# Small additions and scale products moved to GpSimd, and a new hand-planned order, in a fused attention and mixing kernel

## The chip, the cores and the metric

The kernel runs on one core of one Trainium2 chip. A core has TensorE (PE in the profile, matrix products and transposes into PSUM; PEld is its loading of weights), VectorE (DVE), ScalarE (ACT), GpSimd (POOL) and SyncE (SP), which mainly issues transfers. Each engine works through its own queue in the order in which the program issued its instructions; semaphores make one engine wait for another. The metric is the device time of one execution in microseconds. Before the change it is 216.95 us, the median of three runs (216.09 to 218.91).

## What is computed

The reference in numpy, cut to what matters; B = 4 batches, H = 4 heads, S = 1088 positions, D = 32, r = 8:

```python
def phi(x):                                   # 8 x 8 products of two sketches
    a = einsum('rd,bhsd->bhsr', S1, x)
    b = einsum('rd,bhsd->bhsr', S2, x)
    return einsum('bhsi,bhsj->bhsij', a, b).reshape(..., 64)
q_p, k_p = phi(q), phi(k)
kv  = einsum('bhsf,bhsd->bhfd', k_p, v)
z   = sum(k_p, axis=2)
num = einsum('bhsf,bhfd->bhsd', q_p, kv)
den = einsum('bhsf,bhf->bhs', q_p, z) + 1e-06
x   = (num / den) as (B, S, 128)
theta = x @ w_theta
y = w_tok_r @ (x * cos(theta)) + w_tok_i @ (x * sin(theta))   # mixes the 1088 positions
u = x + y
out = u + maximum(u @ w_ch, 0)
```

The denominator comes near zero for some positions, so the kernel keeps it in several exact pieces of the number ("levels"); w_tok arrives as 64-bit floats and is unpacked on the chip.

## The kernel before

Positions are cut into nine chunks of 128 (NC = 9, the last one padded), and three chunks make a group. Per batch the kernel goes through these stages, named here as the plan names them:

- **loads** of K, Q and V (576 KB each) on SP's queue, the first two K on ACT's; for batches 1 to 3 K is loaded a second time (loadh), and a rounded copy is added to it by a GpSimd transfer (`join`, L326).
- **grid / keys / sums / rest**: `key_sums` (L610) squares K on ACT, sums the squares over the partitions on PE, and takes from the sum a grid of powers (`key_grid`, L632: two products on ACT, then their negatives on GpSimd). K is rounded and split on DVE, and PE forms K'K per head in many small products.
- **kT / kf / kv**: `kfeatures` (L700): K transposed, sketched, its 64 features formed on DVE (one outer product per group), and kv summed on PE.
- **chain / kvb**: `chain` (L768) turns K'K into the vector z of the denominators in exact pieces; it reads the grid `kg`. `chain_out` (L866) makes the small factors `mk` and the epsilons `ep` on GpSimd.
- **qscale / qT / q0**: `query_scale` (L918) finds a power of two for Q: square on ACT, sum on PE, bits on DVE, and a product by 2^-49 on ACT (L938), which gives `qs`. `query_slices` transposes Q and multiplies it by `qs` on ACT, and DVE splits it in two.
- **levels / den**: `levels` (L966) multiplies Q with the sketches and with z on PE, then forms the denominators on DVE. `finish_den` (L1011) adds the epsilon, adds the two halves of the denominator (both 128x36) and takes the reciprocal, which then divides the first sketch.
- **num / theta / mix / out**: `outputs_x` (L1023) forms the features of Q (DVE), transposes them (PE), multiplies them with kv, and makes the angles, cosines and sines. `mix_row` (L1193) mixes the positions of batches 0 and 1 with 17 rows of w_tok (`row0` to `row16`, each 1088 KB, unpacked by two instructions of ACT and two of DVE); batches 2 and 3 share seven products instead of eight (`winograd`, L1287: m1 to m7, sums of weights ac1 to ac4). At the end of each comes u @ w_ch, the relu, a transpose and the store.

The work of all these stages is first recorded as 1003 steps ("op": an engine, a planned time, a function, and the buffers that it writes and reads). No scheduler runs: `ORDER` (L34) is the order of all steps, written out by hand or found beforehand, and `Layout.issue` walks through it. So the position of a step in `ORDER` sets its place in its engine's queue. `SLOTS` (L80) gives each buffer its place in eight classes of memory (22 "big" of 128x1152 floats, 5 "zs", 5 "hf", 8 PSUM banks "ps" and so on); a step that opens a buffer waits for the last users of that place. [...]

```python
GAPS = {11: 3, 57: 3, 79: 3, 110: 1, 203: 8, 153: 1, 77: 5, 86: 2, 163: 1}
...
for o in self.order:
    for _ in range(GAPS.get(o.i, 0)):
        fill()
    ...
    o.fn()
```

Most operations are issued through helpers, so that their lines in the profile are those of the helpers: L312 for two-input operations, L316 for tensor with scalars, L319 for both, L332 for matmuls.

Of the kernel before, what the change touches and what calls it, by code (L numbers as in the profile page):

```python
# [245 lines left out]
def kernel(  # L246
# [64 lines left out]
    def tt(eng, o, a, b, f):  # L311
        eng.tensor_tensor(out=o, in0=a, in1=b, op=f)  # L312
# [21 lines left out]
    def bc(x, axis, shape):  # L334
        return x.unsqueeze(axis).to_broadcast(shape)
# [274 lines left out]
    def key_sums(b):  # L610
# [20 lines left out]

        def key_grid():  # L632
            A.mul(kg[b]()[:, 0:1], pg()[:, 0:1], 2.0**5)
            A.mul(kg[b]()[:, 1:2], pg()[:, 0:1], 2.0**14)

        op("A", 0.28, key_grid, [(kg[b], 0)], [pg])
        op("G", 0.2, lambda: ts(kg[b]()[:, 2:4], kg[b]()[:, 0:2], -1.0, ALU.mult, eng=G), [(kg[b], 1)], [(kg[b], 0)], lk=1)

        def key_step():
            x = km()[:, 0:1]  # L640
            ts(x.bitcast(I32), km()[:, 1:2].bitcast(I32), 1, ALU.logical_shift_right)
            ts(x, x, 2.0**76, ALU.mult)

# [274 lines left out]
    def query_scale(b):  # L918
# [13 lines left out]
        def scale():  # L932
            ai = m()[:, 1:2].bitcast(I32)
            ts(ai, ai, 1, ALU.logical_shift_right, EXPO, ALU.bitwise_and)
            ts(ai, ai, EXPO, ALU.bitwise_xor)

        op("V", 0.36, scale, [m], [], lk=2)
        op("A", 0.2, lambda: A.mul(s()[:, 0:1], m()[:, 1:2], 2.0**-49), [(s, 0)], [m])  # L938

    def query_slices(b):  # L940
        at("qT", b)
# [537 lines left out]
```

## Time and profile before

| | |
|---|---|
| median of three runs | 216.95 us |
| the profiled execution | 215.9 us |
| its span, first to last instruction | 214.1 us |
| granted TensorE clock, mean | 0.999 |
| moved by transfers | 37.06 MB, 173 GB/s in the mean |

The profile is of one execution. Its page gives the busy time of each engine, then the span in 40 slices with the busy tenths of each, then the chain of work that ended last. Groups of instructions read: line, engine, operation, output tile <- input tiles, shapes, count | busy microseconds, mean nanoseconds of one | idle time before them and what ended it. Timeline rows read: start, duration, engine, line, operation, tiles, shapes, count, and in brackets the engine's idle time before and what ended it. A matmul of 32-bit floats stands in two records, so the 2140 records of PE are fewer instructions. As matmuls are pipelined and their ends modelled, a busy PE may hide short stalls.

### The profile page before, as it was taken

What the parts mean: (1) busy time and instruction counts of PE and PEld (TensorE: products, weight loads), DVE (VectorE), ACT (ScalarE), POOL (GpSimd) and SP (SyncE); (2) the same over time, 40 slices, a digit from 0 to 9 for tenths busy, and PEclk for the clock granted to TensorE, in tenths of its full rate; (3) what the DMA queues carried; (4) which work ended last, traced back from release to release, by engine and by line L of the source; (5) the groups of instructions that cost most, each with busy time, mean ns of one, the idle gap of its engine ahead of it and who ended that gap; (6) DMA issues with size and microseconds to landing.
All of it is one profiled execution on the core that took longest, in us unless ns stands there. A gap on an engine that the chain in (4) does not pass through costs nothing.

```text
span 214.1 us, 5301 instructions
## 1 busy us (share of the span) xinstructions
PE 207.0 (97%) x2140; PEld 149.7 (70%) x2140; DVE 180.7 (84%) x359; ACT 113.4 (53%) x240; POOL 37.2 (17%) x87
## 2 busy tenths in 40 slices
PE   7899999999999999999999999999999999999992
PEld 7677798968867676775665776666676776676682
DVE  1799999999999998997999999988579599995232
ACT  4899999999998986697531333149700000000000
POOL 1272740306400000840003010000040020020002
PEclk9999999999999999999999999999999999999999
DMA  6999999996996994093000443120590011213503
GB/s 222 393 417 418 384 368 418 420 341 120 357 281 214 431 423 201 29 330 72 0 0 7 69 117 106 32 39 22 174 161 0 0 40 27 40 37 52 92 0 67
DMA packets 28780, 37.06 MB, mean 173 GB/s; under 512 B 21332, under 2 KB 23812, under 8 KB 26580
## 3 DMA queue, kind: packets, MB, share of 16 engines
q1 hardware_dynamic: 23268, 31.91, 42.7%
q0 software_dynamic: 1488, 3.15, 7.0%
q10 hardware_dynamic: 4000, 1.67, 3.0%
q8 instruction: 17, 0.28, 0.5%
q14 instruction: 7, 0.06, 0.1%
HBM read 29.84 MB, written 4.00 MB: 158 GB/s over the span
## 4 chain that ended last, share of the span: by engine, by line
PE 55%; DVE 18%; issue 11%; ACT 6%; DMA 6%; POOL 1%; SPq 1%; POOLq 0%; DVEq 0%; ACTq 0%
PE ps L332 49%; DVE big L312 7%; DMA zs<-far 3%; DMA st<-s 2%; PE ps L1053 2%; PE ps L951 2%; ACT big L626 2%; DVE big L319 1%; DMA far<-zs 1%; DVE g L312 1%; DVE zs L312 1%; DVE big L316 1%; ACT g L726 1%; PE ps L361 1%; POOL out L1236 1%
## 5 line engine op out<-in xcount | busy, mean ns | idle before, releaser
L332 PE MATMUL ps<-big,zs 128*128 128x384 f32 (+2 forms) x380 | 108.9, 435 | 0.3 <-DVE zs L312 0.3
L332 PEld LDWEIGHTS ps<-big,zs 128*128 128x128 f32 x380 | 67.1, 190 | 34.8 <-issue 0.9
L1277 ACT COPY g<-ps 80x256 f32<-80x256 f32 x1 | 0.4, 368 | 55.4 <-PE ps L1270 55.4
L332 PE MATMUL ps<-big,big 128*32 128x32 f32 (+2 forms) x352 | 21.8, 234 | 0.0
L312 DVE CUSTOM_DVE_ANT_0 big<-big,big 128x2176 uint16<-128x2176 uint16 x17 | 21.6, 1282 | 0.1
L578 ACT ACTIVATE big<-zs 128x1088 int32<-128x1088 uint32 (+1 forms) x18 | 21.4, 1193 | 0.4 <-DVE g L312 0.4
L576 ACT ACTIVATE big<-zs 128x1088 f32<-128x1088 f32 x17 | 20.8, 1225 | 0.7 <-DVE lv L312 0.5
L332 PEld LDWEIGHTS ps<-big,big 128*32 128x32 f32 (+1 forms) x352 | 14.9, 124 | 5.6 <-issue 1.0
L312 DVE TENSOR_TENSOR big<-big,big 128x544 f32<-128x544 f32 x24 | 16.7, 714 | 0.1
L326 POOL DMA_DIRECT2D g<-big x6 | 5.3, 1071 | 56.2 <-ACT g L1213 56.2
L312 DVE TENSOR_TENSOR zs<-zs,g 128x384 f32<-128x384 f32 (+2 forms) x24 | 9.9, 450 | 4.7 <-DMA zs<-far 4.7
L1236 POOL DMA_DIRECT2D out<-g x6 | 3.8, 633 | 49.7 <-DVE g L1240 31.8
L316 DVE TENSOR_SCALAR big<-big 128x1088 int32<-128x1088 int32 x17 | 12.3, 721 | 0.0
L361 PE MATMUL ps<-idle 128*128 128x112 bf16 (+1 forms) x67 | 10.0, 312 | 1.3 <-POOL idle L363 1.3
L312 DVE TENSOR_TENSOR g<-lv 128x768 f32<-128x768 f32 x12 | 11.2, 950 | 0.1
L312 DVE TENSOR_TENSOR big<-big,hf 128x1152 f32<-128x1152 f32 x8 | 10.7, 1351 | 0.0
L332 PE MATMUL ps<-mf,big 128*128 128x96 f32 (+1 forms) x72 | 10.0, 277 | 0.4 <-DVE big L312 0.4
L332 PE MATMUL ps<-sbk,g 128*128 128x64 f32 x72 | 10.0, 276 | 0.3 <-ACT g L726 0.3
L332 PE MATMUL ps<-w,big 128*128 128x128 f32 (+1 forms) x76 | 10.2, 278 | 0.0
L1139 ACT ACTIVATE g<-g 128x384 f32<-128x384 f32 x12 | 6.3, 531 | 6.9 <-DVE g L319 6.9
L332 PEld LDWEIGHTS ps<-w,big 128*128 128x128 f32 (+1 forms) x76 | 9.4, 189 | 0.5
L332 PEld LDWEIGHTS ps<-sbk,g 128*128 128x128 f32 x72 | 9.0, 191 | 0.8 <-ACT g L726 0.6
(198 smaller groups left out, 352.9 us busy)
## 6 DMA issues: line engine op xcount, KB each, us to landing
zs<-w_tok SPq DMA_DIRECT2D x17, 1088.0 KB, 10.6
big<-k_l SPq DMA_DIRECT2D x5, 576.0 KB, 12.5
big<-v_l SPq DMA_DIRECT2D x4, 576.0 KB, 15.5
big<-q_l SPq DMA_DIRECT2D x3, 576.0 KB, 10.4
big<-hf POOLq DMA_DIRECT2D x3, 576.0 KB, 10.1
far<-zs SPq DMA_DIRECT2D x3, 576.0 KB, 4.4
zs<-far SPq DMA_DIRECT2D x12, 144.0 KB, 4.2
big<-k_l ACTq DMA_DIRECT2D x2, 576.0 KB, 4.4
```

The source lines that it names most:

```text
L312: eng.tensor_tensor(out=o, in0=a, in1=b, op=f)
L316: (eng or V).tensor_scalar(out=o, in0=a, scalar1=s1, scalar2=s2, op0=op0, **kw)
L326: op("G", 0.9, lambda: G.dma_start(dst(), src(), accum_op=ALU.add), w, r, fly=fly)
L332: T.matmul(o, lhs, rhs, start=start, stop=stop, skip_group_check=True)
L361: T.matmul(nowhere()[:, :n], idle()[:, 0:P], idle()[:, :n], start=True, stop=True, skip_group_check=True)
L576: op("A", 0.22 + n * 0.0009, lambda: A.activation(dfn(), words_of(raw(), n)[1].bitcast(F32), AF.Prelu, scale=2.0**-112, alpha=-(2.0**32)), ...
L578: op("A", 0.22 + n * 0.0009, lambda: A.activation(stp(), words_of(raw(), n)[0].bitcast(U32), AF.Copy, scale=2.0**-29), [stp], [raw])
L626: op("A", act(n) + 0.1, lambda: A.activation(flat(r()), kc(), AF.Square, accum_out=km()[:, 1:2]), [r, (km, 1)], [kx])
L951: T.transpose(tr()[:, i * P:(i + 1) * P], x()[:, g * GC + i].rearrange("p h d -> p (h d)"), ident())
L1053: T.transpose(tr()[:, i * P:(i + 1) * P], qp()[:, i * H + 2 * n:i * H + 2 * n + 2].rearrange("p h i j -> p (h i j)"), ident())
L1139: op("A", act(GW), lambda cs=cs: A.activation(cs()[:, 0], cs()[:, 1], AF.Abs), [(cs, 0)], [(cs, 1)])
L1236: E.dma_start(out[b, s0:s0 + n, f * SQ:(f + 1) * SQ].rearrange("(c j) i -> j c i", j=SQ), ot()[f * SQ:(f + 1) * SQ, :n].rearrange("j (c i) ...
```

## The change

Four things are edited.

1. `key_grid` keeps one product on ACT; the second grid value is made from the first by a GpSimd product (by 2^9), in front of the negatives, which were there already.
2. The product by 2^-49 in `query_scale` goes from ACT to GpSimd.
3. The two additions of `finish_den` go from DVE to GpSimd; the reciprocal becomes a step of its own on DVE. This adds one step per batch, 1007 in all, so that later steps have higher numbers in the new `ORDER`.
4. `ORDER` and `SLOTS` are replaced. The first 58 entries of `ORDER` are the same. `GAPS` is untouched; its keys are all below the first new step.

```diff
         pg = buf("ps", (512,), F32, "pg")
         op("P", 0.25, lambda: mm(pg()[:, 0:1], ones(), km()[:, 1:2], True, True), [pg], [(km, 1)])

-        def key_grid():
-            A.mul(kg[b]()[:, 0:1], pg()[:, 0:1], 2.0**5)
-            A.mul(kg[b]()[:, 1:2], pg()[:, 0:1], 2.0**14)
-
-        op("A", 0.28, key_grid, [(kg[b], 0)], [pg])
-        op("G", 0.2, lambda: ts(kg[b]()[:, 2:4], kg[b]()[:, 0:2], -1.0, ALU.mult, eng=G), [(kg[b], 1)], [(kg[b], 0)], lk=1)
+        def more_grid():
+            ts(kg[b]()[:, 1:2], kg[b]()[:, 0:1], 2.0**9, ALU.mult, eng=G)
+            ts(kg[b]()[:, 2:4], kg[b]()[:, 0:2], -1.0, ALU.mult, eng=G)
+
+        op("A", 0.2, lambda: A.mul(kg[b]()[:, 0:1], pg()[:, 0:1], 2.0**5), [(kg[b], 0)], [pg])
+        op("G", 0.7, more_grid, [(kg[b], 1)], [(kg[b], 0)], lk=2)
...
-        op("A", 0.2, lambda: A.mul(s()[:, 0:1], m()[:, 1:2], 2.0**-49), [(s, 0)], [m])
+        op("G", 0.5, lambda: ts(s()[:, 0:1], m()[:, 1:2], 2.0**-49, ALU.mult, eng=G), [(s, 0)], [m], lk=1)
...
         def finish_den():
             d1 = dn()[:, 1].rearrange("p (c h) -> p c h", h=H)
-            tt(V, d1, d1, bc(ep[b]()[:, 1], 1, [P, NC, H]), ALU.add)
-            tt(V, dn()[:, 0], dn()[:, 0], dn()[:, 1], ALU.add)
-            V.reciprocal(dn()[:, 1], dn()[:, 0])
-
-        op("V", 0.8, finish_den, [dn], [(ep[b], 1)], lk=2)
+            tt(G, d1, d1, bc(ep[b]()[:, 1], 1, [P, NC, H]), ALU.add)
+            tt(G, dn()[:, 0], dn()[:, 0], dn()[:, 1], ALU.add)
+
+        op("G", 0.55, finish_den, [dn], [(ep[b], 1)], lk=2)
+        op("V", 0.4, lambda: V.reciprocal(dn()[:, 1], dn()[:, 0]), [dn], [])
...
 ORDER = (
     0, 1, 29, 32, 4, 2, 5, 3, 34, 30, 356, 50, 33, 102, 44, 96, 6, 108, 103, 36, 7, 51, 366, 54, 144, 8, 97, 10, 9,
     11, 55, 109, 20, 52, 12, 57, 139, 58, 59, 60, 61, 62, 63, 126, 13, 31, 132, 56, 98, 127, 264, 14, 391, 128, 143,
-    245, 15, 145, 64, 65, 67, 68, 78, 35, 69, 16, 70, 19, 148, 149, 150, 151, 152, 268, 99, 66, 79, 246, 53, 80, 100,
...
+    245, 15, 145, 129, 99, 16, 104, 268, 130, 120, 100, 133, 246, 257, 78, 64, 65, 66, 105, 110, 111, 258, 19, 67, 53,
...
```

In the new order, behind the shared opening, the key features of batches 0, 1 and 3 (kT, kf, kv) come ahead of the small products of batch 0 (sums, rest), those of batch 1 (sums) come after them, and the squares of Q2 and K2 on ACT come ahead of the first unpacked row. On SP's queue the second copies of K2 and K3 and part of Q3 come earlier, and rows 11, 13, 15 and 16 of w_tok come last. Later, 41 instead of 36 mixing steps of batches 0 and 1 stand ahead of the levels of batch 3 on PE. At the very end the last output pieces of batches 2 and 3 change places: m4 instead of m3 is the last product.

103 rows, old and new, of tables (ORDER, SLOTS) are left out of this document.

## The prediction

> **What bounds the kernel now.** I read the page first, then the busy time in ten-microsecond windows, then what TensorE waited for, then the timeline of the places that the edits touch. From the page:
>
> ```profile
> span 214.1 us, 5301 instructions
> PE 207.0 (97%) x2140; PEld 149.7 (70%) x2140; DVE 180.7 (84%) x359; ACT 113.4 (53%) x240; POOL 37.2 (17%) x87
> PE   7899999999999999999999999999999999999992
> DVE  1799999999999998997999999988579599995232
> ACT  4899999999998986697531333149700000000000
> PE 55%; DVE 18%; issue 11%; ACT 6%; DMA 6%; POOL 1%; SPq 1%; POOLq 0%; DVEq 0%; ACTq 0%
> ```
>
> TensorE (PE) is busy nearly to the last slice. VectorE (DVE) is as full as PE for the first 120 us, and ScalarE (ACT) for the first 85 us. So the chain that ended last is shared by two engines that are both full, and an instruction taken off DVE or ACT pays only where PE was waiting for it. The windows (columns PE, PEld, DVE, ACT, POOL, PEclk, DMA share, GB/s) say the same:
>
> ```profile
> 10.00:20.00 10.00, 9.72 (x204) 7.86 (x204) 9.62 (x20) 9.88 (x26) 4.85 (x17) 1.00 1.02 417
> 110.00:120.00 10.00, 9.59 (x64) 6.65 (x63) 9.90 (x16) 2.08 (x4) 1.82 (x2) 1.00 0.24 40
> 160.00:170.00 10.00, 10.00 (x42) 6.69 (x41) 8.06 (x16) 0.00 (x0) 0.00 (x0) 1.00 0.00 0
> ```
>
> The granted clock is 1.00 throughout. After 125 us DVE has room and PE alone sets the time. What PE still waits for, in all 214.1 us:
>
> ```profile
> PE ps L361 <- POOL idle L363: 1.3, 1, 1.3
> PE ps L415 <- DVE m L434: 0.8, 1, 0.8
> PE ps L332 <- DVE big L312: 0.4, 1, 0.4
> PE ps L332 <- ACT g L726: 0.3, 1, 0.3
> PE ps L332 <- DVE zs L312: 0.3, 1, 0.3
> PE ps L332 <- DVE hf L316: 0.2, 1, 0.2
> PE ps L1270 <- DVE big L319: 0.2, 1, 0.2
> ```
>
> These are 3.5 us. The first two (2.1) and the wait for hf L316 (0.2, the keys of batch 0) lie in the opening, whose 58 plan entries are the same in both orders; the last of them on PE is the transpose at 11.44 in the rows below. 1.2 us are left to win. PE also holds work that computes nothing, the fillers of L361:
>
> ```profile
> L361 PE MATMUL ps<-idle 128*128 128x384 bf16 x28 | 6.2, 327 | 0.0
> L361 PE MATMUL ps<-idle 128*128 128x112 bf16 x39 | 3.8, 300 | 1.3 <-POOL idle L363 1.3
> 11.44 0.50 PE L723 MATMUL ps<-ident,big 128*128 128x128 f32 x3
> 14.37 1.46 PE L361 MATMUL ps<-idle 128*128 128x384 bf16 x8
> ```
>
> GAPS is unchanged, and the steps that its keys name are the same: the fillers stay, 6.2 + 3.8 = 10.0 us (eight of them in one stretch at 14.37), whether the new order needs them there or not.
>
> **The change, part by part.** The sum is made against the profiled execution: 215.9 us, of which 214.1 are span and 1.8 lie around it. It is 1.05 below the median of the runs, 216.95; that is added at the end.
>
> 1. Denominators. Two additions of 128x36 leave DVE's finish_den in each of four batches and go to GpSimd (POOL); the reciprocal stays on DVE as a step of its own.
>
> ```profile
> L312 DVE TENSOR_TENSOR sm<-sm 128x36 f32<-128x36 f32 x4 | 0.8, 197 | 0.1
> L312 DVE TENSOR_TENSOR sm<-sm,sm 128x36 f32<-128x36 f32 x4 | 0.8, 194 | 0.0
> 94.63 0.21 ACT L938 ACTIVATE qs<-sm 128x1 f32<-128x1 f32 x1
> 94.92 0.19 POOL L312 TENSOR_TENSOR qs<-qs 128x1 f32<-128x1 f32 x1 [2.72 <-ACT qs L938]
> 95.19 0.19 POOL L312 TENSOR_TENSOR qs<-qs,ec 128x1 f32<-128x1 f32 x1
> ```
>
> DVE is relieved of 4 x (0.194 + 0.197) = 1.6 us. POOL has no row of 128x36; the nearest are these small additions: a hand-over of about 0.1 (94.63 + 0.21 to 94.92), 0.27 to the next start, 0.19, and a hand-over back, about 0.65 in all. The reciprocal is queued on DVE behind other work in the new order: for batch 0 behind the split of chain 1 and one outer product, for batch 1 behind one phase product only, for batch 2 behind six conversions and additions of weight rows, for batch 3 behind one stream transpose. The covers' rows:
>
> ```profile
> 74.16 0.96 DVE L312 TENSOR_TENSOR g<-lv 128x768 f32<-128x768 f32 x1
> 88.48 1.36 DVE L1097 STREAM_TRANSPOSE zs<-big 128x1152 f32<-128x1152 f32 x1
> 86.53 1.35 DVE L312 TENSOR_TENSOR big<-big,hf 128x1152 f32<-128x1152 f32 x1
> 86.61 2.04 POOL L316 TENSOR_SCALAR mf<-mf 128x64 f32<-128x64 f32 x1
> ```
>
> So 0.65 is hidden in all four if POOL runs freely. It may not: the 2.04 us of POOL L316 began right after a DVE operation of 1.35 and lasted beyond it. If the cover itself holds POOL off, DVE waits the 0.65 after it in batches 0, 1 and 3: 2.0 us. It can't be more in one place, as DVE then issues nothing that could hold POOL further. Bounds for DVE: 1.6 gained to 0.4 lost. I take 1.6 less one such wait of 0.65 (batch 1, with the shortest cover): 0.9 gained on DVE. Behind the waiting reciprocal stands DVE's whole queue, next the product that PE's transposes of the query features need.
>
> [...]
>
> 2. Scale products of keys and queries. ACT loses the second product of key_grid and the product of L938, four of each; POOL gains them.
>
> ```profile
> L634 ACT ACTIVATE kg<-ps 128x1 f32<-128x1 f32 x4 | 0.7, 181 | 0.0
> L938 ACT ACTIVATE qs<-sm 128x1 f32<-128x1 f32 x4 | 0.9, 224 | 0.0
> L316 POOL TENSOR_SCALAR kg<-kg 128x2 f32<-128x2 f32 x4 | 2.1, 530 | 11.1 <-ACT kg L634 11.0
> ```
>
> ACT gains 0.7 + 0.9 = 1.6. On POOL each costs 0.53 in the mean. The key grid is due some microseconds later (chain of its batch) and nobody notices. The query scale is needed by ACT's scaled copies of the transposed queries; in the new order three of four stand far enough behind, and batch 2 asks for its scale soon after DVE made it, so ACT may wait once, 0 to 0.53 (2.04 if held as above). I take 0.5. ACT gains 1.1.
>
> 3. Order and slots. All 1003 steps remain (1007 with the split), no matmul and no transfer is added, so PE's busy work is the same. Adding up the durations of the rows ahead of a step on its own queue, first to last, shows what moves. Before, the last level matmuls of batch 3 wait for the last subtraction of its queries:
>
> ```profile
> 117.62 1.64 PE L332 MATMUL ps<-mf,big 128*128 128x96 f32 x12 [0.41 <-DVE big L312]
> 100.46 4.03 PE L332 MATMUL ps<-big,zs 128*128 128x320 f32 x12 [0.27 <-DVE zs L312]
> 18.97 0.88 PE L332 MATMUL ps<-sbk,g 128*128 128x64 f32 x6 [0.28 <-ACT g L726]
> ```
>
> In the new order 41 mixing steps instead of 36 stand on PE ahead of that level step (3.0 us more PE work), and 1.5 us more work on DVE ahead of the subtraction: the wait of 0.41 goes with 1 us to spare. The same count, taken for each PE step against the DVE or ACT step that it needs, leaves PE 0.8 us or more to spare from 12 us on, and about 2 from 50 us on. So the waits of 0.4, 0.3, 0.3 and 0.2 go: 1.2. What is late next is DVE and ACT, which in several places now stand behind PE by 1 to 4 us; that costs nothing while they have the spare time that PE leaves them. SP's queue: the loads of K2's copy, Q3 and K3's copy go ahead of V1, V3 and row 0, and rows 11, 13, 15 and 16 are loaded last through two staging buffers.
>
> ```profile
> zs<-w_tok SPq DMA_DIRECT2D x17, 1088.0 KB, 10.6
> 90.86 0.33 SPq L575 DMA_DIRECT2D zs<-w_tok  x1
> 97.78 1.21 ACT L578 ACTIVATE big<-zs 128x1088 int32<-128x1088 uint32 x1
> ```
>
> Row 15 may not be issued before ACT has unpacked row 11, so ACT can wait a few microseconds near 95 us, where it has room. I cost it at nothing; the cover is the work on DVE and the mixing steps of other rows, and if it is gone, each row late by the 10.6 us of a busy queue instead of the 7 us of a free one (issued at 90.86, unpacked from 97.78) costs 3.7.
>
> Sum: 215.9 - 1.2 (PE's waits) - 0.8 (of 0.9 on DVE and 1.1 on ACT I let 0.4 each reach PE, since in the first 120 us they set PE's pace only in places) + 0.5 (new small waits) = 214.4; with 1.05 to the median 215.4.
>
> **Rivals.**
> - Nothing moves, 216.9 (chance 0.24). PE was full, fillers stay, and 1.2 us of waits come back in other places. For it: 97% busy; against it: the spare time counted above.
> - All of it arrives, 212.4 (0.08). PE's 1.2, DVE's 1.6 and ACT's 1.6 all reach the end: 216.95 - 4.4. For it: the 120 us in which all three are full; against it: after 125 us PE is full without them.
> - GpSimd becomes the wait, 221.5 (0.07). Held additions and products: 2.0 on DVE, and four query scales at 2.04 less 0.22 each, 7.3 on ACT, of which the first two of the densest part (3.6) would reach PE; less the 1.2 of waits: +4.5. It decides from about 1 us per query scale on. Against it: POOL is busy 17%.
> - The last weight rows come late, 221 (0.05): two rows, 3.7 each, less what the mixing of batch 1 hides (2 to 3).
>
> [...] The page has 17 packets on one instruction queue, 0.28 MB, and the largest group of waits for nothing visible is that of PE's weight loads:
>
> ```profile
> q8 instruction: 17, 0.28, 0.5%
> PEld ps L332 <- issue: 5.2, 17, 0.6
> ```
>
> None of those is longer than 0.6 us, and weight loads run ahead of the matmuls, so program fetches get no case. [...]
>
> **How the numbers follow.** The forecast of 215.4 has 0.56; its own range is 214 to 216.5 (no new small waits and 0.9 more of DVE's and ACT's gain, or three times the new waits). With the case of 216.9 beside it 0.80 lie between 212.8 and 219.5, which is the range: it leaves out 0.08 below and 0.12 above, and its ends stand for all gains less the new waits (216.95 - 4.4 + 0.5 = 213.05, rounded outward) and for one such place as 2.0 on DVE in the third rival, with no wait of PE removed (218.95, rounded outward). Two per cent is 4.3 us, about what a measurement of this kernel can tell from no change (its three runs lie 2.8 apart). Faster by more: 0.08, the second rival. Slower by more: 0.11, the third (0.07) and most of the fourth (0.04). Between: 0.81.
>
> **What would show it.** Right: PE's waits after 12 us under 0.5 us in all; DVE at L1018 (the reciprocal) idle under 0.7 before each; PE busy share 98%. Wrong: idle time of DVE released by POOL of over 1 us at a reciprocal, ACT idle for POOL's qs, PE idle for rows of weights near 105 to 115 us, or PE's mixing steps after 125 us beginning later than now.

## The result and the profile after

The changed kernel takes 222.97 us (median of 6 runs, 222.56 to 223.34), the kernel before 216.69 beside it (6 runs): a ratio of 1.0281, interval 1.0230 to 1.0332. The prediction said 215.4 within 212.8 to 219.5; it was wrong, in size and in sign. Ratios here leave out executions that took over 1.5% more than the fastest of the same kernel, so where a kernel's times scatter the ratio tells the least that it loses, and the range of all runs stands beside it.

The profiled execution of the changed kernel took 222.57 us, with a span of 220.8 against 214.1. Its lines are those of before plus one from the moved products on (L332 is L333 here, L361 is L362). First its page, then TensorE's waits:

```profile
span 220.8 us, 5295 instructions
PE 209.7 (95%) x2140; PEld 152.8 (69%) x2140; DVE 180.9 (82%) x351; ACT 113.7 (52%) x232; POOL 46.1 (21%) x103
PEclk9999997999999999999999999999999999999999
```

```profile
PE ps L333 <- issue: 3.5, 4, 1.3
PE ps L362 <- POOL idle L364: 1.3, 1, 1.3
PE ps L416 <- DVE m L435: 0.9, 1, 0.9
PE ps L333 <- ACT sm L931: 0.7, 1, 0.7
PE ps L333 <- DVE hf L317: 0.2, 1, 0.2
```

Two things are new. "issue", a wait for nothing that the profile shows, is now on TensorE's matmuls, four times, 3.5 us; before it was on weight loads alone, 0.6 at the most. And the granted clock, which was full before, dips in the seventh slice. The waits of 0.4, 0.3 and 0.3 for DVE and ACT that the prediction wanted gone are gone, and one of 0.7 for ACT is new.

Where the 6.7 us of span lie: TensorE is busy 2.7 longer (209.7 against 207.0) and idle 4.0 longer. The listed waits explain 3.1 of the idle time (6.6 here, 3.5 before). The chain of waits between 24 and 60 us gives the places of the four stalls (start, length, what):

```profile
29.00 1.26 issue
42.10 0.54 issue
48.24 0.82 issue
54.76 0.84 issue
```

All of them lie between 29 and 56 us, and in the six microseconds ahead of each stand clusters of tiny matmuls (32 outputs, 32 or 64 columns). What TensorE waits for does not appear as an instruction. It appears in the DMA queues. Two answers of the DMA view, for the stretches 27.9 to 28.9 us and 28.9 to 33.5 us of the changed kernel (queue, packets, MB, share of 16 engines):

```profile
DMA packets 59, 0.30 MB, mean 296 GB/s; under 512 B 8, under 2 KB 8, under 8 KB 46
...
q8 instruction: 1, 0.02, 6.0%
```

```profile
DMA packets 1198, 1.61 MB, mean 350 GB/s; under 512 B 884, under 2 KB 884, under 8 KB 1183
...
q1 hardware_dynamic: 1143, 1.43, 93.8%
q0 software_dynamic: 55, 0.18, 15.3%
```

q8, an instruction queue by its name, is read here as TensorE's program, because the number of its packets follows TensorE's records: 17 of 16 KB each beside 4280 matmuls and weight loads, 14 in the two runs below that leave out 640 of these, 18 in the two that add 464. One packet fills 6.0% of 16 engines for 1.0 us, so one engine for 0.96: it runs from 27.93 to 28.89, and TensorE goes on at 30.26, 1.37 later. The next four microseconds hold none. The other three stalls end in the same way: packets that end at 41.27, 47.71 and 54.18, and matmuls that start at 42.64, 49.06 and 55.60, 1.37, 1.35 and 1.42 later.

Matmuls, weight loads and the semaphore records of TensorE counted together give the places. The four stalls begin about 961, 1473, 1730 and 1985 instructions into the program, and those of the same order with the operations on their old engines (second experiment) again at 961, 1473 and 1730, and at 1217. The distances are 512, 257 and 255, and 256 from 961 to 1217, so the program is counted here in blocks of 256, one packet each. Late in the kernel before, where the data queues are nearly empty (DMA share 0.10 to 0.27 around these packets), a packet starts about 290 instructions ahead of the use of its block (285, 294 and 279 for the packets at 127.4, 143.7 and 173.7 us); this point is called due below. Between 20 and 54 us, where the data queues are full (DMA share 0.97 to 1.06), in the changed kernel it starts 3.5 to 7.1 us after that point. By this count there is no stall where these 290 instructions last as long as this delay, 1.0 of transfer and the 1.4 from a packet's end to the next matmul together. In the kernel before, between 19 and 64 us, the delay was 1.7 to 6.5 us, and the packets ended 1.8 to 5.1 us ahead of their use, all of it over the 1.35 to 1.42 after which the stalls ended: it had no stall, but only by 0.4 us at 60 us.

The half clock is seen in three stretches of 3.41 us of the changed kernel (busy time of PE, PEld, DVE, ACT, POOL, then the granted clock, DMA share and GB/s):

```profile
29.13:32.54 3.41, 2.28 (x24) 2.06 (x23) 2.06 (x8) 1.31 (x3) 0.44 (x2) 1.00 1.02 377
32.54:35.95 3.41, 3.41 (x92) 2.95 (x90) 3.34 (x7) 2.57 (x6) 3.22 (x6) 0.50 1.01 225
35.95:39.36 3.41, 3.41 (x61) 3.02 (x60) 1.86 (x4) 2.08 (x5) 3.12 (x7) 1.00 0.99 381
```

The stretch with the stall of 1.26 (TensorE busy 2.28 of 3.41) is followed by one at half clock. If everything in it ran at half speed, 3.41 us would do the work of 1.7; this estimate of at most 1.7 is set against the 2.7 by which busy time grew. It is an upper bound, as the matmuls of 32 outputs took 241 and 314 ns there against 196 and 219 elsewhere.

### The profile page after: what moved, and what is told of

It reads as the page before. It is cut to its first block, busy times and chain, and to the rows that moved or that the text cites. A ratio compares the mean times of both kernels' runs of the same rounds, so it can differ in the third digit from the quotient of the medians.

```text
span 220.8 us, 5295 instructions
## 1 busy us (share of the span) xinstructions
PE 209.7 (95%) x2140; PEld 152.8 (69%) x2140; DVE 180.9 (82%) x351; ACT 113.7 (52%) x232; POOL 46.1 (21%) x103
## 4 chain that ended last, share of the span: by engine, by line
PE 68%; issue 12%; DVE 9%; DMA 7%; ACT 1%; POOL 1%; POOLq 0%; DVEq 0%
PE ps L333 62%; DVE big L313 6%; DMA big<-q_l 5%; DMA st<-s_t 2%; PE ps L1054 2%; PE ps L362 2%; PE ps L952 1%; DVE big L320 1%; DVE zs L313 1%; POOL out L1237 1%; DVE g L1241 1%; PE ps L1127 1%; PE ps L724 1%; ACT big L627 1%; ACT big L577 0%
## 5 line engine op out<-in xcount | busy, mean ns | idle before, releaser
L333 PE MATMUL ps<-big,zs 128*128 128x384 f32 (+2 forms) x380 | 107.9, 434 | 0.0
L333 PEld LDWEIGHTS ps<-big,zs 128*128 128x128 f32 x380 | 67.3, 190 | 35.1 <-issue 0.9
L333 PE MATMUL ps<-big,big 128*32 128x32 f32 (+2 forms) x352 | 22.3, 240 | 0.8 <-issue 0.8
L333 PEld LDWEIGHTS ps<-big,big 128*32 128x32 f32 (+1 forms) x352 | 14.9, 130 | 6.8 <-issue 2.1
L333 PEld LDWEIGHTS <-hf 128*32 128x32 bf16 (+1 forms) x252 | 8.3, 100 | 6.5 <-issue 4.7
L362 PE MATMUL ps<-idle 128*128 128x112 bf16 (+1 forms) x67 | 10.2, 315 | 1.3 <-POOL idle L364 1.3
L333 PE MATMUL ps<-w,big 128*128 128x128 f32 (+1 forms) x76 | 10.6, 280 | 0.0
L333 PE MATMUL ps<-mf,big 128*128 128x96 f32 (+1 forms) x72 | 10.4, 279 | 0.0
L333 PEld LDWEIGHTS ps<-w,big 128*128 128x128 f32 (+1 forms) x76 | 9.6, 189 | 0.8
L333 PE MATMUL ps<-sbk,g 128*128 128x64 f32 x72 | 9.8, 273 | 0.0
L333 PEld LDWEIGHTS ps<-mf,big 128*128 128x128 f32 (+1 forms) x72 | 8.8, 185 | 0.7
```

What stands on the lines that cost most here:

```text
L333: T.matmul(o, lhs, rhs, start=start, stop=stop, skip_group_check=True)
L362: T.matmul(nowhere()[:, :n], idle()[:, 0:P], idle()[:, :n], start=True, stop=True, skip_group_check=True)
```

## The experiments

Every time is beside the kernel before on the same chip (216.6, 216.0, 215.84 and 216.66 us in four batches). Theory F is that the program fetches come late. Its rivals are G (GpSimd's new work holds the others up), O (the new order makes engines wait for each other) and, later, R1 and R2, which the texts state.

**Which half of the change.** One run has the moves without the order, one the order without the moves.

```diff
 e1: the moves to GpSimd kept
-ORDER, SLOTS = new
+ORDER, SLOTS = those of before, the reciprocal one DVE step later
 e2: ORDER, SLOTS = new
-additions and products on GpSimd
+additions and products on DVE and ACT, as before
```

> The moves to GpSimd with the old order and slots (each reciprocal stands one DVE step later in batches 0 to 2, directly behind the additions in batch 3). Theory F (TensorE's program is fetched too late behind the loads in the new order, and its clock drops after the idle stretch): 216 to 217.5 us, no wait of TensorE for nothing visible of over 0.3 us, clock at 1.00. Theory G (GpSimd's additions and products hold DVE and ACT up): 220 us or more. Theory O (the new order makes engines wait for each other, fetches apart): 216 to 217.5.

> The new order and slots with the additions on DVE and the products on ACT as before. Theory F: 222 to 224 us, TensorE waits 3 us or more for nothing visible between 25 and 60 us, in stretches of 0.5 us and more, each ending about 1.4 us after a 16 KB packet of the instruction queue has landed, and the clock is halved for some 3 us. Theory G: 217 or less. Theory O: 222 to 224, but with waits that name DVE, ACT or a load.

The moves alone: 217.43, ratio 1.0022 (0.9996 to 1.0048). The order alone: 223.74, ratio 1.0314 (1.0257 to 1.0371), with the same signature among TensorE's waits:

```profile
PE ps L334 <- issue: 4.1, 4, 1.4
```

So the moves cost 1.0 us at most by the interval, and the order is the loss.

**Emptier data queues.** An eighth of each row of w_tok is loaded and used eight times, in either kernel.

```diff
-SY.dma_start(raw(), src)
+SY.dma_start(raw()[:, :n // 8], src[:, :n // 8])   # and the unpacking reads it 8 times
```

> The kernel before, with an eighth of each of the 17 rows of w_tok loaded and used eight times over (so the output is not the reference's): 16 MB less traffic, the same work on every engine. A control for the next run. All theories: 214 to 216.5 us, since TensorE is full.

> The changed kernel with the same eighth of each row loaded. Theory F: the instruction packets are no longer behind full queues, TensorE's waits for nothing visible fall below 1 us in all and the clock stays at 1.00; the time lies within 2 us of the light kernel before, 214 to 217.5. Theory O and theory G: the distance between the two light kernels stays 4 us or more, 219 or more.

The kernel before: 215.04, ratio 0.9938 (0.9919 to 0.9957). The changed one: 218.28, ratio 1.0052 (1.0005 to 1.0099), and no wait of TensorE for "issue" is left in it. Between 20 and 60 us its program packets start 0.5 to 3.4 us after the point at which they are due, where they started 3.5 to 7.1 after it. The distance falls from 6.3 to 3.2 us: F had asked for 2 at the most, G and O for 4 or more, so the fetches are shown to be a part of the loss and not all of it. In the profiled execution (217.06 us) no wait for fetches is in what is left; of the 2.1 us between the two profiled spans (213.2 and 215.3) 1.4 is busy time of TensorE, whose clock is at half from 212.9 us to the end.

**More instructions in the same order.** 29 groups of eight matmuls of 32x32 are put between the steps of the kernel before, once with full rows and once with light ones.

```diff
+            if o.i in EXTRA:            # 29 steps between about 17 and 41 us
+                for j in range(8):
+                    fill(32, 32 * (j % 4))
```

> The kernel before with its old order and its old loads, with 29 x 8 extra matmuls of 32x32 outputs between about 17 and 41 us that write a bank nobody reads (464 more instructions of TensorE, about 0.07 us of work for eight: 2 us). F: a block now lasts 4.5 to 5.5 us there, so the packets come too late here too: waits for nothing visible of 1.5 to 5 us at the first matmul behind a packet, time 220 to 224. Rival R2 (the new order's loads hold the fetches up, the density of instructions does not matter): only the added work, 218 to 219.5, no such waits.

> The same extra matmuls in the kernel before with an eighth of each weight row loaded and used eight times (its output is then not the reference's). The data queues are emptier and the packets start about 1 us after they are due. F: no waits for nothing visible; 215.0 of the same kernel without the extra matmuls plus their own work, 216.5 to 217.5. The time of the run with full rows less this one, less 1.6 (what light rows alone are worth), is what the late fetches cost: F 2 to 5 us, R2 0.

Full rows: 231.26 and 234.23 us, with two more runs at 238.79 and 239.40. Light rows: 220.56, ratio 1.0194 (1.0133 to 1.0255). The same instructions in the same order cost 11 to 14 us more, by the two shorter runs, when the data queues are full; 1.6 of that is what light rows save anyway. Both times lie above what F had said. The profiled executions are 11.7 us of span apart (229.5 and 217.8). TensorE's waits, first with full rows, then with light ones:

```profile
PE ps L336 <- issue: 4.3, 4, 2.0
PE ps L336 <- DVE zs L316: 1.7, 1, 1.7
```

```profile
PE ps L336 <- issue: 0.7, 1, 0.7
```

and the clock with full rows:

```profile
PEclk9999797999999999799999999999999999999998
```

The differences in these waits are 5.3 us, and three stretches of 3.41 us at half clock with full rows are worth at most 5.1 more by the estimate above. R2 (only the added work) is out, as the stalls come with the old order and its loads. My price of that work was not right either: 5.5 us (220.56 less 215.04) instead of 2.

**Spliced orders, and instructions left out.** With the moves kept, the old order was used up to a step and the new one behind it, or the reverse (each splice has places for its buffers, `SLOTS`, of its own):

```diff
-ORDER = new
+e5: old order for 400 steps (61 us), then the new one
+e6: new order for 300 steps (45 us), then the old one
+e7: new order for 120 steps (25 us), then the old one
+e12: new order for 120 steps, old one to step 560 (96 us), then the new one
```

> The moves to GpSimd with the old order for its first 400 steps (to about 61 us on TensorE) and the new order for what is left. Theory F (program fetches): TensorE's program comes in blocks of 256 matmuls and weight loads, one packet each; in the new order a block lasts about 5.0 to 5.5 us of work between 24 and 56 us, in the old one 6 to 8, and while the data queues are full the packet of the next block comes too late for 5.4. With the old order in that stretch no stall remains: TensorE's waits for nothing visible under 0.5 us in all before 60 us, time 216.5 to 218. Rival R1 (the late part of the new order costs it: the last weight rows through two staging buffers, or steps of DVE and ACT behind TensorE after 61 us): 219.5 or more.

> The opposite: the new order for its first 300 steps (to about 45 us on TensorE), then the old order. F: the waits at the blocks that begin near 29, 42 and 48 us come back, 2 to 4 us together, time 219 to 222. R1: the late part is the old one, so 217 to 218.

> With the moves to GpSimd, the new order in its first 120 steps (to about 25 us on TensorE), then the old order. The opening is where the changed kernel was ahead by 0.8 us, and no block of the old order behind it lasts under 5 us. F: 216 to 218, no waits for nothing visible over 0.5; better than before by up to 0.8 if the seam adds no wait. R1 has no different number.

> The new order for 120 steps, the old one to step 560 (about 96 us), the new one to the end: with the moves, the opening and the late part of the change, without its dense stretch. Between 86 and 124 us the kernel before loses 2.1 us of TensorE's time and the changed one 0. F: 214.5 to 217. R1 (late part costs): 219 or more.

e5 222.3 (ratio 1.0263, 1.0210 to 1.0315), e6 225.82 (1.0446, 1.0389 to 1.0503), e7 220.93 (1.0242, 1.0177 to 1.0308), e12 226.91 (1.0529, 1.0468 to 1.0590). F's statements on fetches held in part: no wait for "issue" in e5 and e7 (and none in e12), but 1.7 us of it at two places in e6, where 2 to 4 at three were expected. All four of its times are misses, while R1's held in e5 and e12 and failed in e6. Each seam has a wait that neither order has at that size, 2.4, 2.7 and 3.3 us in e5, e6 and e12.

```profile
64.49 0.92 PE L334 MATMUL ps<-big,big 128*32 128x32 f32 x64 [2.37 <-DMA big<-hf]
```

```profile
PE ps L1055 <- DVE g L314: 2.7, 1, 2.7
```

```profile
105.92 6.26 PE L334 MATMUL ps<-big,zs 128*128 128x320 f32 x14 [3.31 <-DVE zs L314]
```

A stretch of half clock follows each of them (granted clock 0.6 in the slice from 65.9 us of e5, 0.7 in those from 50.4 of e6 and 106.8 of e12), and in e7 several waits of 0.2 to 0.7 are followed by one of 6.83 us. The splices therefore do not tell F from R1; they suggest that a wait of TensorE for an engine or a load can be paid a second time through the clock, as by the same reading the stall of 1.26 for the program was.

In the other pair most products of the rest steps are left out, 320 matmuls with as many weight loads:

```diff
-heads(1, x, kc()[:, c * HD:(c + 1) * HD])
+if not c: heads(1, x, kc()[:, c * HD:(c + 1) * HD])   # likewise for the other products of these steps
```

> The changed kernel without all but the first chunk of the products of the rest steps in all four batches (its output is then not the reference's): some 500 TensorE instructions fewer, with only about 2 us of work in them (16 of them take 0.07 us). F (a program block must last longer than its fetch): blocks last longer, TensorE's waits for nothing visible and the half clock behind them go, so far more than the 2 us of work is gained: 214 to 217.5. Rival R1 (the loss lies in DVE, ACT and the loads of the new order): only the work, 220 to 221.5.

> The control: the same products left out of the kernel before. It has no such stalls, so both theories expect the work alone: 213.5 to 215.5. F expects the distance of the two kernels to shrink from 6.3 to 1 to 3 us, R1 expects 5.5 to 6.5.

The changed kernel: 223.98, ratio 1.0344 (1.0281 to 1.0407); the kernel before: 216.59, ratio 1.0038 (0.9999 to 1.0076). Both misses: neither gained the work that was left out, and the distance of the two did not shrink (6.6 us by the ratios, where F said 1 to 3 and R1 5.5 to 6.5). In the changed kernel one late packet still cost 2.5 us, and TensorE ran into a wait of 3.3 for ACT at 21 us:

```profile
21.23 0.40 PE L333 MATMUL ps<-psc,sx 8*128 8x64 f32 x2 [3.29 <-ACT sm L932]
45.05 0.38 PE L953 MATMUL ps<-ident,big 128*128 128x128 f32 x2 [2.53 <-issue]
```

So the mean density of instructions is not the measure. With 640 instructions left out, all later ones stand elsewhere in the blocks, and the kernel before now waits 1.0 for "issue" too. That made the next question: does the position of the blocks alone move the time?

**The blocks shifted, nothing else.** The fillers (matmuls of zeros into a bank that nobody reads) that run before the first data arrive are cut into more or fewer pieces of about the same columns in all. Order, loads, steps and their work are the same; each step stands a fixed number of places further on, or back, in the blocks.

```diff
-[spin(112) for _ in range(39)]
+[spin(61) for _ in range(71)]    # e13, kernel before: 64 instructions more
+[spin(384) for _ in range(11)]   # e14, kernel before: 56 fewer
+[spin(190) for _ in range(23)]   # e15, changed kernel: 32 fewer
+[spin(50) for _ in range(87)]    # e16, changed kernel: 96 more
```

> The kernel before, with its 39 opening fillers of 112 columns replaced by 71 of 61: the same columns of work before the first data arrive, but 64 more TensorE instructions, so that every later step stands 64 places further in the program's blocks. Order, loads and steps are the same. F, worked out by the block positions (a block is asked for 290 instructions ahead of its use, starts 4.5 us later, lands 1 us later, and TensorE goes on 1.4 us after that, on the instruction times of the run with light rows): stalls of 2.9 near 38 us and 1.2 near 57 us instead of 0.5, 219 to 222 with some half clock behind them. The order itself as the cause (R1): 216 to 217.

> The kernel before with 11 opening fillers of 384 columns instead of 39 of 112: 56 instructions fewer ahead of every step. F by the same count: stalls of 0.7 near 42 us and 1.0 near 56 us, 217.5 to 219.5. R1: 216 to 217.

> The changed kernel with 23 opening fillers of 190 columns: 32 instructions fewer ahead of every step. F by the same count: stalls of 0.5, 1.3 and 0.8 (2.5 us) near 30, 39 and 50 us instead of 3.5, 220 to 222.5, and the wait of 1.26 near 30 us gone or under 0.7. R1: 222.5 to 223.5, as the changed kernel.

> The changed kernel with 87 opening fillers of 50 columns: 96 instructions more ahead of every step. F by the same count: stalls of 1.1, 0.7 and 3.4 (5.5 us) near 19, 31 and 41 us, 224 to 228. R1: 222.5 to 223.5.

| run | stalls counted beforehand, us (near) | stalls measured, us (until) | all runs, us (the profiled one) | ratio to before |
|---|---|---|---|---|
| e13 | 2.9 (38), 1.2 (57) | 0.99 (14), 1.89 (42), 1.32 (65) | 220.43 to 225.25 (224.21) | 1.0188 (1.0131 to 1.0245) |
| e14 | 0.7 (42), 1.0 (56) | 0.58 (43) | 217.48 to 225.44 (217.76) | 1.0072 (1.0033 to 1.0111) |
| e15 | 0.5 (30), 1.3 (39), 0.8 (50) | 0.99 (42), 1.05 (49), 0.61 (55) | 221.54 to 227.62 (221.54) | 1.0273 (1.0189 to 1.0357) |
| e16 | 1.1 (19), 0.7 (31), 3.4 (41) | 0.73 (21), 0.56 (33), 3.45 (46) | 225.82 to 227.21 (225.82) | 1.0451 (1.0407 to 1.0494) |

The kernel before is slowed by 1.9% without a change in any step, and the changed kernel, 1.0281 as it is, goes to 1.0451. The cutting of the fillers costs little by itself: the short wait of TensorE for DVE that follows them (0.23 us) ends at 8.73 to 8.99 us in the four, 8.72 in the kernel before. R1 expected all four to stay where they were. Only e15 misses F's time (222.6 by the ratio, 220 to 222.5 expected) and agrees with R1's, while its wait near 30 us is gone, as F expected; three others of 2.65 us in all stand in it. The second stall counted for e14 did not come, and e13 has one at 14 us that was not counted. The largest stall, in e16, on the chain of waits:

```profile
42.42 3.45 issue
45.87 0.95 PE ps L333 x19
```

the packet behind which it ends, in the DMA view of 43.6 to 44.65 us (it ends at 44.63, 1.24 ahead of the 45.87 above):

```profile
DMA packets 61, 0.36 MB, mean 346 GB/s; under 512 B 6, under 2 KB 6, under 8 KB 36
...
q8 instruction: 1, 0.02, 5.9%
```

and what the clock does behind it, in stretches of e16:

```profile
40.87:44.28 3.41, 1.55 (x52) 1.15 (x41) 1.68 (x4) 1.86 (x5) 2.56 (x8) 1.00 1.02 320
44.28:54.52 10.24, 8.65 (x124) 8.51 (x127) 5.28 (x11) 4.92 (x9) 1.21 (x2) 0.50 1.00 337
```

The stall of 3.45 is followed by 10.24 us at half clock, with TensorE busy for 8.65 of them: by the estimate above at most 4.3 us of work lost once more.

## Why the prediction was wrong

- The failed step is the sentence on program fetches: "None of those is longer than 0.6 us, and weight loads run ahead of the matmuls, so program fetches get no case." It judged a resource by the waits that it had caused so far, and not by its margin. Weight loads did start ahead of their matmuls (82.26 against 82.37 us in the kernel before), but no run shows that this hides a late packet of the program: four stalls of the changed kernel, 3.5 us, ended 1.35 to 1.42 us behind one. The view of the queues and the windows would have given a margin: 17 packets for 2140 matmuls and as many weight loads are 252 instructions each, data queues full between 10 and 50 us (DMA share 1.00 to 1.03), and the instructions in a stretch of ten microseconds as a price. The windows from 25 to 35 us show the difference. Before, then after:

```profile
25.00:35.00 10.00, 9.99 (x171) 8.89 (x171) 9.42 (x21) 9.34 (x24) 2.58 (x11) 1.00 1.02 369
```

```profile
25.00:35.00 10.00, 8.74 (x207) 7.60 (x206) 7.99 (x21) 6.49 (x17) 6.15 (x16) 0.88 1.06 331
```

  342 instructions before and 413 after, although TensorE stood still for 1.26 us of it. Five packets between 20.0 and 53.25 us, one in 6.65, bring 385 in ten. But one window does not decide it: the next one of the kernel before has 481, more than either, and no stall. There the packets started 3.0 and 4.3 us after they were due, and their margin held.

```profile
35.00:45.00 10.00, 10.00 (x241) 8.83 (x240) 9.76 (x25) 9.63 (x27) 1.75 (x5) 1.00 1.02 415
```

- Step 3 said that the new order "leaves PE 0.8 us or more to spare from 12 us on". Against DVE and ACT that was nearly right: one new wait of 0.7 (ACT sm L931), and behind 85 us the old waits are gone. Adding up the durations on each queue could not see a wait whose producer is not an instruction. The sum's -1.2 came; +3.5 of stalls and at most 1.7 of half clock came on top and were in no term. The sum's -0.8 rested on less busy time of DVE and ACT, and neither fell (180.9 against 180.7 and 113.7 against 113.4). At least 1.9 of the 6.7 us (1.0 busy, 0.9 in idle pieces that the list of waits leaves out) are assigned to nothing here.
- Step 1 was right in its mechanism. DVE waits 0.2 once at the reciprocal, where 0.65 once was taken and 2.0 was the bound; the two additions cost 0.69 and 0.33 on GpSimd, 1.0 together where 0.65 was taken with the hand-overs, and nearly all of it was hidden. But DVE's busy time did not fall by 1.6:

```profile
L1018 DVE RECIPROCAL sm<-sm 128x36 f32<-128x36 f32 x4 | 1.4, 362 | 0.2 <-POOL sm L313 0.2
L313 POOL TENSOR_TENSOR sm<-sm 128x36 f32<-128x36 f32 x4 | 2.7, 685 | 0.3
L313 POOL TENSOR_TENSOR sm<-sm,sm 128x36 f32<-128x36 f32 x4 | 1.3, 331 | 27.7 <-DVE sm L1008 25.7 <-DVE sm L313 2.0
```

  It is 180.9 against 180.7, with eight instructions fewer; why was not tried. With the old order it is 179.7.
- Step 2 costed 0.53 a product and one wait of 0.5 for ACT; the scale products took 0.62 and 0.51 in the mean, and the list of ACT's waits has none for GpSimd. The third rival (GpSimd becomes the wait, 221.5) came near the time by a wrong way: e1 has the same GpSimd work and 217.43.
- The fourth rival (last rows of weights late) did not come: no wait of TensorE lies behind 85 us.
- "What would show it" asked for waits after 12 us under 0.5 us in all and a busy share of 98%: 4.2 us and 95% say wrong, and the list of waits by itself points to a reason that was not on the list.

What is shown and what is not. That late packets make the stalls is shown by their ends, by e4, and by e8 against e9; that the position of the blocks moves the stalls and the time is shown by e13 to e16. That position alone makes the difference between the two orders is not shown: in no position tried does the changed kernel come under a ratio of 1.0273. That the half clock is caused by the stalls ahead of it is argued from their order in time alone, as no run changed the clock by itself, and the traces do not bear it out as a rule. A stretch with TensorE busy 2.28 of 3.41 us was followed by half clock, but in e2 one with a stall of 1.39 was not, and in e15 half clock follows a stretch in which TensorE was busy throughout. First e2, then e15:

```profile
39.90:43.31 3.41, 2.02 (x105) 1.61 (x98) 3.13 (x9) 2.26 (x7) 3.11 (x7) 1.00 1.01 300
43.31:46.72 3.41, 3.41 (x80) 3.10 (x68) 1.74 (x7) 2.74 (x9) 0.00 (x0) 1.00 1.02 340
```

```profile
26.85:30.26 3.41, 3.41 (x64) 2.87 (x64) 3.31 (x10) 2.67 (x7) 1.74 (x9) 1.00 1.03 344
30.26:33.67 3.41, 3.41 (x87) 3.33 (x86) 3.24 (x9) 1.89 (x6) 2.49 (x4) 0.50 1.08 342
```

So the tiny matmuls of the new order may lower the clock without a stall; no run separates the two. The remaining 3.2 us between the two kernels with light rows are open in part.

## What to carry to other kernels

Here the program was a load too, 17 packets of 16 KB. Where a stretch is full of tiny matmuls and the DMA queues are full at the same time (413 instructions in ten microseconds at a DMA share of 1.06 in the changed kernel), count the instructions per microsecond against the packets of the instruction queue before an order is changed, and ask by how much each packet was early, not whether anything waited. When a change that moves no work makes a tuned kernel slower, shift the program by some dozens of instructions in a place that costs nothing: here 32 to 96 places gave other stalls in all four runs, and moved the ratio by up to 1.9% (e13) and 1.7% (e16). Keep large loads out of the stretches with many small instructions (light rows took all waits for fetches, 3.5 us, out of the changed kernel); spreading the small instructions instead was not tried.

## What the runs showed of the hardware

- TensorE resumed 1.20 to 1.60 us after the end of the program packet that it waited for, in all 27 stalls of 0.4 us or more that the traces have.
- In the changed kernel a packet of the program started up to 7.1 us after it was due while the DMA share was about 1.0 (10.4 once in e16), and 0.5 to 3.4 us after with light rows.
- The half clock came in stretches of 3.41 us or multiples (6.83, 10.24), after stretches in which TensorE was busy 2.28 or 1.55 of 3.41 us, but also all 3.41. So neither a stall nor the busy share orders the cases. A measure that does, but for one, is the size of the matmuls. Count each matmul as its columns (twice for 32-bit floats) times the share of 128x128, the largest operand in the traces, that its weights fill, and add this up over stretches of 3.41 us at full clock, between 11 and 205 us of all 18 traces: all 15 sums under 2,600 were followed by half clock, and of the 989 larger ones only the one in e15 (2,872). The weights were chosen after the fact, so this describes these runs and is no rule.
- Eight matmuls of 32x32 outputs with their weight loads cost 0.17 us of the end time (5.5 us for 29 groups, less 0.7 of stall) where rows of eight small matmuls with their weight loads (32 outputs, starts at 11.87, 11.94 and 12.00 us of the kernel before) had suggested 0.07.
